# Where one pair's loads stand in the sync engine's queue: an attention and Mish feed-forward kernel in units of three head pairs

## The chip, the cores and the metric

The kernel runs on one core of a Trainium2 chip, and all eight batches are done by that core. The metric is the device time of one execution in microseconds (us), as the median of several runs.

A core has a matrix engine (PE in the profile; PEld is its weight load), a vector engine (DVE), a scalar engine (ACT), a general one (POOL) and a sync engine (SP) that here does nothing but issue DMAs. Each engine works through its own queue in order, and the engines wait for each other through semaphores. All loads of q, k and v, all transposes that are done by DMA and nearly all stores are issued by SP, one behind the other.

## The reference

The kernel computes attention with one extra unit in the denominator of the softmax, and feeds its output, regrouped to one row per token, to a two-layer network with the Mish activation. In and out are float32; B, H, S, D are 8, 12, 448, 64, d_model is 768 and d_ff is 2048.

```
scale = 1.0 / np.sqrt(q.shape[-1])
scores = scale * np.matmul(q, k.transpose(0, 1, 3, 2))
m = np.max(scores, axis=-1, keepdims=True)
e = np.exp(scores - m)
attn = e / (np.sum(e, axis=-1, keepdims=True) + np.exp(-m) + 1e-09)
attn_out = np.matmul(attn, v)

x = attn_out.transpose(0, 2, 1, 3).reshape(B * S, H * D)
h = x @ w_in
g = h * np.tanh(np.log1p(np.exp(h)))      # h itself for the softplus where h > 20
out = g @ w_out
```

## The kernel before, in words

**Pairs and units.** Two heads are a pair; a batch has six pairs, and there are 48. Three pairs are a unit (`UNIT_PAIRS`), two units a batch, so there are 16 units with attention work, u = 0 to 15. The first six pairs (u = 0 and 1) go one by one. The loop `for u in range(UNITS_PER_B, ...)` (line 726) then works on several stages at once: in the pass of unit u it does the scores and exponentials of unit u, the product with v for the pairs of unit u - 1, the first feed-forward product with Mish for part of an earlier batch (`mm1_mish`, L442 and L481), and pieces of the second feed-forward product (`mm2_group`, L548), which fill PE wherever the attention steps wait. In the text a unit is called by its u; the fifth unit is u = 4.

**A pair's way.** `load_pair` (line 149) issues three loads on SP, q, k and v of the pair, 224 KB each (L158), into buffers of which there are four of each kind. `cast_pair` (line 190) casts them to bfloat16 on POOL: q (L201 or L203), k (L207) and v (L188). q and k are then transposed, by PE (`transpose_pair`, L224), or, for the first pair of each unit from pair 21 on and for pair 46, by a DMA on SP (`turn_by_dma`, L237, here called the turn; `TURN_BY_DMA` lists these pairs). The scores (L304, L307, L312) are reduced to maxima by DVE (L335), and ACT takes the exponentials e and their sums (L347). When all e of a unit are there, `normalise` (line 369) divides by the denominator, on DVE (L386), for the third pair of a unit on POOL (L384). It then issues the transpose of that pair's e on SP (L390), so that e can be multiplied by v (`av_pair`, L423).

**A unit's two parts.** The first part is the scores and exponentials. From u = 6 on (`JOINED_FROM`) its order is written out by hand in `JOINED` (line 630): "s" is a score product, "m" the maxima, "e" the exponentials, "fill" a piece of the second feed-forward product, "copy" and "store" its results, "av" and "avc" the product with v of unit u - 1 and its copy, and "cast", "turn" and "load" the steps named above, for the pairs of the next units. The three "av" stand near the end of the order, the one with the third pair (`("av", 2)`) last; score products and exponentials follow behind it. For u = 4 and 5 the orders `GROUPED_LATE_AV` and `LOAD_AT` play that part. The second part is the loop `for f in range(FF_U)` (line 857), eight first feed-forward products with Mish. Between them stand the three normalisations and e transposes of unit u: the first at f = 0, the second at f = 3, the third at f = 4. In the same loop, at f = 1, 3 and 5, PE transposes q and k of those pairs of the next unit that aren't turned by DMA.

**The order on SP in one unit before the change.** For u from 7 on it is: the turn of the next unit's first pair (`("turn", 0)`); the loads of two pairs (`("load", 0)`, p0 + 4, and `("load", 1)`, p0 + 5, where p0 is the unit's first pair); the stores; the loads of one more pair (`("load", 2)`, p0 + 6, the first pair of the unit after the next); and then the three e transposes. `cast_pair` for p0 + 6 stands at the opening of the next unit (`("cast", 0)`). In u = 6 the loads are one pair behind (`lead`), and the pair that closes the row is loaded behind the turn at the end of the order (line 778). In u = 5 the three pairs are loaded at n = 0, 3 and 6 of the first part (line 807).

Of the kernel before, what the change touches and what calls it, by code (L numbers as in the profile page):

```python
# [15 lines left out]
UNIT_PAIRS = 3  # L16
# [3 lines left out]
def kernel(  # L20
# [97 lines left out]
    JOINED_FROM = 2 * UNITS_PER_B + 2  # L118
# [30 lines left out]
    def load_pair(p, which="qkv"):  # L149
        if p >= N_PAIRS:  # L150
            return
        b, h0 = p // HP, (p % HP) * 2
        tiles = loaded.setdefault(p, [])
        for nm, src in (("q", q), ("k", k), ("v", v)):
            if nm not in which:
                continue
            t = ld_pool.tile([SP_, 2, NT * D], FP32, tag=f"{nm}_f", name=f"{nm}_f")
            nc.sync.dma_start(  # L158
                out=t, in_=src[b, h0 : h0 + 2].rearrange("h (p t) d -> p h (t d)", t=NT)
            )  # L160
            tiles.append(t)
# [28 lines left out]
    def cast_pair(p, with_v=True):  # L190
        if p >= N_PAIRS:
            return
        q_f, k_f = loaded[p][:2]
        q_bf, k_bf = (qk_bf[:, p % N_CAST, i] for i in range(2))
        v_bf = bf_pool.tile([SP_, 2, NT * D], BF16, tag="v_bf", name="v_bf")
        by_t = "p h (t d) -> p t h d"
        cast_q, cast_k = nc.gpsimd.tensor_copy, nc.gpsimd.tensor_copy
        if p == 0:
            cast_q, cast_k = nc.vector.tensor_copy, nc.scalar.copy
        if p not in SCALED_IN_CAST:  # L200
            cast_q(out=q_bf, in_=q_f.rearrange(by_t, t=NT))  # L201
        else:
            nc.gpsimd.tensor_scalar(  # L203
                out=q_bf, in0=q_f.rearrange(by_t, t=NT),
                scalar1=SCALE, scalar2=1.0, op0=ALU.mult, op1=ALU.mult,
            )
        cast_k(out=k_bf, in_=k_f.rearrange(by_t, t=NT))  # L207
        casted[p] = (q_bf, k_bf, v_bf)
        if with_v:
            cast_v(p)  # L210
# [32 lines left out]
    def rest_of(p):  # L243
        qT, q_rest = qkT[p][0], q_rests[p % UNIT_PAIRS]
        nc.gpsimd.tensor_copy(out=q_rest[0:64, 0, :], in_=qT[0:64, 384:S])
        nc.gpsimd.tensor_copy(out=q_rest[64:128, 1, :], in_=qT[64:128, 0:64])
# [324 lines left out]
    first_mm2 = 2 * UNITS_PER_B  # L571
# [5 lines left out]
    for g in range(B // 2):  # L577
# [50 lines left out]
        [],  # L628
    )
    JOINED = (  # L630
        ("mA", 1), ("cast", 0), ("fill", 2), ("mA", 0), ("fill", 1), ("mB", 0), ("fill", 1),
        ("eA", 1), ("mB", 1), ("fill", 2), ("eA", 0), ("mB", 2), ("fill", 1), ("eB", 1),
        ("mA", 2), ("fill", 2), ("eB", 0), ("fill", 1), ("copy", 0), ("fill", 3), ("eB", 2),
        ("fill", 3), ("s", 3), ("turn", 0), ("load", 0), ("eA", 2), ("fill", 1), ("m", 3),
        ("s", 5), ("s", 4), ("s", 6), ("mA", 5), ("e", 3), ("fill", 1), ("mA", 6), ("fill", 1),
        ("eA", 5), ("load", 1), ("fill", 1), ("mB", 5), ("fill", 1), ("eA", 6), ("fill", 1),
        ("mB", 4), ("s", 7), ("fill", 2), ("m", 7), ("eB", 4), ("fill", 1), ("mA", 4),
# [18 lines left out]
    BY_POOL = 3  # L656
    LEAD = UNIT_PAIRS + 1
    LOAD_AT = (0, 3, 6)
    TURN_AFTER = (8, 11)
    LAST_AV_AT = 9  # L660
    HEAD = HP
# [64 lines left out]
    for u in range(UNITS_PER_B, N_UNITS + 2 * UNITS_PER_B):  # L726
# [16 lines left out]
        for what, arg in JOINED if joined else ():  # L743
            at, idx = p0 + arg, p0 * STEPS + arg
            heads = {"A": (0,), "B": (1,)}.get(what[-1], (0, 1))
            if what == "s":
                held[arg] = score_products(idx)
            elif what[0] == "m":
                score_maxima(*held[arg], heads)
            elif what[0] == "e":  # L750
                exps(idx, heads)
            elif what == "fill":
                for _ in range(arg):
                    filler.popleft()[0]()
            elif what == "store":
                while to_store:
                    store_rows(*to_store.pop(0))
            elif what == "copy":
                for evac in copies[arg]:
                    evac()  # L760
            elif what == "av":
                held["av", arg] = av_pair(at - UNIT_PAIRS, bank=joined_banks[AV_BANK[arg]])
            elif what == "avc":
                held["av", arg]()
            elif what == "cast":
                if u > JOINED_FROM:
                    cast_pair(nxt)
            elif what == "load":
                lead = LEAD - 1 if u == JOINED_FROM else LEAD
                load_pair(at + lead)  # L770
                if arg:
                    cast_pair(at + lead - 1)
            elif u > JOINED_FROM:
                if nxt + arg in TURN_BY_DMA:
                    turn_by_dma(nxt + arg)
            elif arg:
                turn_by_dma(nxt)
                load_pair(nxt + UNIT_PAIRS)
        if joined:
            expm_of(nxt - 1)  # L780

        for n in () if joined else range(steps):
            pi, s = divmod(n, STEPS)
            p, idx = p0 + pi, p0 * STEPS + n
            late_tp = u == UNITS_PER_B and n == STEPS
            if late_tp:
                transpose_pair(p0 + 2)
            exps(idx)
            if grouped:
                order = GROUPED_LATE_AV if u in LATE_AV else GROUPED  # L790
                flush_late()
                for what, arg in order[n]:
                    if what == "fill":
                        for _ in range(min(arg, len(filler))):
                            fn, w = filler.popleft()
                            fn()
                            done += w
                    elif what in ("av0", "av1"):
                        late.append(av_pair(p0 - UNIT_PAIRS + arg, bank=sc_banks[int(what[2])][0]))
                    else:  # L800
                        flush_late()
                        for i in arg:
                            scores(p0 * STEPS + i)
                if n in LOAD_AT:
                    at = p0 + LOAD_AT.index(n)
                    if u > first_mm2:
                        load_pair(at + LEAD - 1)
                        if n:
                            cast_pair(at + LEAD - 2)
                    elif n < LOAD_AT[-1]:  # L810
                        load_pair(at + LEAD)
                        cast_pair(at + LEAD - 1)
                if u - UNITS_PER_B < len(W_AT):
                    load_w(W_AT[u - UNITS_PER_B].get(n, 0))
                if n in TURN_AFTER and nxt + TURN_AFTER.index(n) in TURN_BY_DMA:
                    turn_by_dma(nxt + TURN_AFTER.index(n))
                continue
            if late_tp:
                evac_qk(p0 + 2, act=True)
            if u == UNITS_PER_B + 1:  # L820
                for i, part in enumerate(TURN_AT[1].get(n, [])):
                    turn_on_pe(*part)
                    if n == 0:
                        mm1_ahead(0, FIRST_AHEAD[i])
            flush_late()
            acc += weight[n]
            want = int(total * acc / sum(weight) + 1e-6)
            while done < want:
                fn, w = filler.popleft()
                fn()  # L830
                done += w
            scores_ahead(end)
            if n in LOAD_AT:
                load_pair(p0 + LOAD_AT.index(n) + LEAD)
                cast_pair(p0 + LOAD_AT.index(n) + LEAD - 1)
            if u - UNITS_PER_B < len(AV_AT):
                early = AV_AT[u - UNITS_PER_B]
                if n in early:
                    late.append(av_pair(early[n], act=early[n] in AV_BY_ACT))
                if u == UNITS_PER_B:  # L840
                    for part in TURN_AT[0].get(n, []):
                        turn_on_pe(*part, act=part in TURN_BY_ACT)
            elif u == N_UNITS and n == LAST_AV_AT:
                for i in range(UNIT_PAIRS):
                    late.append(av_pair(p0 - UNIT_PAIRS + i, bank=sc_banks[i][0]))
            if u - UNITS_PER_B < len(W_AT):
                load_w(W_AT[u - UNITS_PER_B].get(n, 0))
# [9 lines left out]
        for f in range(FF_U):  # L857
# [38 lines left out]
            if f == 3:  # L896
                normalise(todo[1], dma=todo[1] not in BY_PE)
                for p in TURN_BY_DMA:
                    if p // UNIT_PAIRS == u + 1:
                        rest_of(p)  # L900
            if f == 4:
                normalise(todo[2], dma=todo[2] not in BY_PE, on_pool=u + 1 < N_UNITS)
        if attn and u + 1 < N_UNITS:
# [38 lines left out]
```

## Time and profile before

| | |
|---|---|
| median of 3 runs | 459.84 us |
| lowest, highest | 458.76, 463.82 us |
| the profiled execution, its own time | 463.51 us |
| its span, first to last instruction | 461.7 us |
| busy: PE, DVE, ACT, POOL | 430.9, 341.3, 342.0, 185.4 us |
| DMA queue q1 (SP and ACT issue to it) | 85.76 MB, 86.8% of 16 engines' span |
| e transposes by DMA (L390) | 43, median 6.5 us from issue to landing |
| loads of q, k, v (L158) | 48 of each, median 5.1, 5.4 and 5.6 us from issue to landing |

A row of the timeline gives the start in us from the beginning of the span, the duration, the engine, the line of the kernel, the operation, what it writes from what, and how many of one kind were merged; idle time of the engine ahead of it stands in brackets with what ended it. "SPq" is SP's queue; the duration of its rows is the time that the issue holds the queue, not the transfer, which is told by the time to landing. The table of waits gives the time in total, how often, and the longest.

### The profile page before, as it was taken

The page shows a single profiled execution, that of the slowest core. Times are in us where ns is not written, and L with a number is a line of the kernel's source. Part 1 is how long each engine was busy: PE and PEld are TensorE (multiplying, and loading weights), DVE is VectorE, ACT ScalarE, POOL GpSimd, SP SyncE. Part 2 cuts the span into 40 slices and gives each one's busy share as a digit, 9 for nine tenths or more (in the row PEclk, how much of TensorE's full clock was granted, in tenths as well). Part 3 has the DMA queues.
Part 4 walks back from the last instruction along what each step waited for, and adds up shares of the span by engine and source line. Part 5 has one row for each costly group of instructions (what it writes and reads, how often), then busy time and mean ns, then how long its engine had stood idle before and what let it go on. Part 6 is the DMA issues. An engine that isn't in the chain of part 4 may idle for free.

```text
span 461.7 us, 8725 instructions
## 1 busy us (share of the span) xinstructions
PE 430.9 (93%) x2968; PEld 237.4 (51%) x2968; DVE 341.3 (74%) x756; ACT 342.0 (74%) x908; POOL 185.4 (40%) x352
## 2 busy tenths in 40 slices
PE   4587899799999999999999899999999999989996
PEld 2243545454544555555545455565555555555565
DVE  4899777989796888878878888888888888321021
ACT  4998887989696989888878688897978888211300
POOL 3666738462607245453618062535435340000000
PEclk9998589999999999999999999999999999999999
DMA  8999999998999999899999999999999996950213
GB/s 217 219 195 224 256 173 236 200 197 201 203 230 250 222 242 213 258 199 258 220 217 261 198 239 197 277 209 261 230 262 203 233 173 138 177 132 0 70 36 102
DMA packets 211660, 92.65 MB, mean 201 GB/s; under 512 B 168352, under 2 KB 208160, under 8 KB 211616
## 3 DMA queue, kind: packets, MB, share of 16 engines
q1 hardware_dynamic: 204032, 85.76, 86.8%
q0 software_dynamic: 7488, 6.29, 9.4%
q8 instruction: 23, 0.38, 0.3%
q14 instruction: 21, 0.17, 0.1%
q10 hardware_dynamic: 96, 0.05, 0.0%
HBM read 45.61 MB, written 11.01 MB: 123 GB/s over the span
## 4 chain that ended last, share of the span: by engine, by line
PE 69%; DMA 11%; ACT 6%; DVE 6%; issue 2%; SPq 2%; POOL 2%; POOLq 0%; ACTq 0%
PE mo L548 23%; PE mo L442 17%; PE b L442 10%; PE b L304 5%; DMA eT<-en 5%; ACT en L347 5%; DVE negm L335 4%; PE b L548 4%; PE mo L423 3%; DMA k_f<-in_k_dram 3%; DMA v_f<-in_v_dram 2%; PE b L224 2%; PE b L423 2%; SPq L390 1%; DMA q_f<-in_q_dram 1%
## 5 line engine op out<-in xcount | busy, mean ns | idle before, releaser
L347 ACT ACTIVATE en<-b,negm 128x448 bf16<-128x448 f32 x216 | 134.2, 642 | 24.1 <-DVE negm L335 24.1
L335 DVE TENSOR_REDUCE negm<-b 128x1 f32<-128x448 f32 x216 | 121.1, 614 | 15.7 <-PE b L307 15.7
L548 PEld LDWEIGHTS <-gT 128*128 128x128 bf16 x896 | 82.2, 98 | 50.2 <-issue 9.1
L548 PE MATMUL mo<-w_out_sb,gT 128*128 128x384 bf16 (+3 forms) x736 | 107.2, 298 | 0.6 <-ACT gT L481 0.6
L442 PEld LDWEIGHTS <-w_in_sb 128*128 128x128 bf16 x768 | 72.2, 98 | 66.6 <-issue 5.6
L442 PE MATMUL mo<-xT,w_in_sb 128*128 128x448 bf16 x480 | 100.9, 353 | 0.7 <-DVE xT L432 0.3
L384 POOL TENSOR_SCALAR en<-en,rden 128x448 bf16<-128x448 bf16 x109 | 67.5, 640 | 30.3 <-DVE rden L378 23.0
L481 ACT ACTIVATE gT<-mo 128x448 bf16<-128x448 f32 x73 | 40.3, 551 | 52.8 <-PE mo L442 52.6
L386 DVE TENSOR_SCALAR en<-en,rden 128x448 bf16<-128x448 bf16 x227 | 71.7, 385 | 0.7
L442 PE MATMUL b<-xT,w_in_sb 128*128 128x448 bf16 x282 | 58.8, 353 | 0.1
L524 DVE COPY o_sb<-mo 128x384 f32<-128x384 f32 (+3 forms) x54 | 25.8, 492 | 41.6 <-PE mo L548 39.9
L201 POOL CAST qk_bf<-q_f 112x512 bf16<-112x512 f32 x29 | 18.2, 628 | 95.0 <-DMA q_f<-in_q_dram 94.7
L347 ACT ACTIVATE en<-sc,negm 128x448 bf16<-128x448 f32 x84 | 52.6, 644 | 3.9 <-DVE negm L335 2.6
L335 DVE TENSOR_REDUCE negm<-sc 128x2 f32<-128x896 f32 (+1 forms) x48 | 45.4, 968 | 7.0 <-PE sc L307 3.7
L347 ACT ACTIVATION_READ_ACCUMULATOR en<-b,negm 128x1 f32 x216 | 46.2, 214 | 0.0
L188 POOL CAST v_bf<-v_f 112x512 bf16<-112x512 f32 x48 | 30.2, 630 | 17.6 <-DMA v_f<-in_v_dram 15.0
L423 PEld LDWEIGHTS <-v_bf 112*64 112x64 bf16 x384 | 20.8, 112 | 24.0 <-issue 14.4
L207 POOL CAST qk_bf<-k_f 112x512 bf16<-112x512 f32 x47 | 29.1, 620 | 4.9 <-DMA k_f<-in_k_dram 4.0
L423 PE MATMUL mo<-eT,v_bf 112*64 112x448 bf16 x232 | 28.0, 373 | 3.3 <-DMA eT<-en 2.8
L224 PEld LDWEIGHTS <-qk_bf 112*128 112x128 bf16 x304 | 20.2, 106 | 18.3 <-DVE qk_bf L201 4.4
L307 PE MATMUL b<-qk_all 64*128 64x448 bf16 x108 | 29.3, 354 | 0.3 <-ACT en L347 0.3
L304 PE MATMUL b<-qk_all 64*128 64x448 bf16 x108 | 29.3, 354 | 0.0
(71 smaller groups left out, 515.8 us busy)
## 6 DMA issues: line engine op xcount, KB each, us to landing
q_f<-in_q_dram SPq DMA_DIRECT2D x48, 224.0 KB, 5.1
k_f<-in_k_dram SPq DMA_DIRECT2D x48, 224.0 KB, 5.4
v_f<-in_v_dram SPq DMA_DIRECT2D x48, 224.0 KB, 5.6
w_in_sb<-in_moe_w_in_dram POOLq DMA_DIRECT2D x12, 256.0 KB, 5.9
w_out_sb<-in_moe_w_out_dram POOLq DMA_DIRECT2D x8, 384.0 KB, 7.3
out_dram<-o_sb SPq DMA_DIRECT2D x7, 336.0 KB, 5.9
out_dram<-o_sb SPq DMA_DIRECT2D x8, 288.0 KB, 4.9
out_dram<-o_sb SPq DMA_DIRECT2D x8, 240.0 KB, 5.5
```

The source lines that it names most:

```text
L188: nc.gpsimd.tensor_copy(out=casted[p][2], in_=loaded.pop(p)[2])
L224: nc.tensor.transpose(by_s[s][:, t * SP_ : (t + 1) * SP_], src[:, t].rearrange("p h d -> p (h d)"), ident[:SP_, :SP_],)
L304: nc.tensor.matmul(sc[0][:, 0:S], lhsT=qT[0:64, qa : qa + 128], rhs=kA, start=True, stop=True)
L307: nc.tensor.matmul(sc[1][:, 0:S], lhsT=qT[64:128, qb : qb + 128], rhs=kB, start=True, stop=True)
L335: nc.vector.tensor_reduce(out=negm, in_=scored, axis=AX.X, op=ALU.max, negate=True)
L347: nc.scalar.activation(out=st["en"][:, :, c, 0:SP_], in_=sc[bk][:, 0:S].rearrange("q (j c) -> q j c", j=NT), func=AF.Exp, bias=st["negm"][ ...
L384: nc.gpsimd.tensor_scalar(scalar2=1.0, op0=ALU.mult, op1=ALU.mult, **args)
L386: nc.vector.tensor_scalar(scalar2=None, op0=ALU.mult, **args)
L423: nc.tensor.matmul(av[h * 64 : (h + 1) * 64, 0:S], lhsT=v_bf[:, h, j * D : (j + 1) * D], rhs=e_h, start=(j == 0), stop=(j == NT - 1),)
L442: nc.tensor.matmul(h_ps[:, 0:S], lhsT=w_in_sb[:, dm, ff * 128 : (ff + 1) * 128], rhs=xT[b][:, dm, :], start=(dm == 0), stop=(dm == DM_T - 1),)
L481: nc.scalar.activation(out=gT[b][:, ff, :], in_=h_ps[:, 0:S], func=AF.Mish)
L548: nc.tensor.matmul(st["o"][:, st["at"] : st["at"] + nq * NQ], lhsT=src[:, ff, c0 : c0 + 128], rhs=w_out_sb[:, ff, q0 * NQ : (q0 + nq) * NQ ...
```

## The change

From u = 4 on, the loads of the pair `nxt + UNIT_PAIRS` (the first pair of the unit after the next, where `nxt` is the first pair of the next unit) are issued at f = 3 of the unit's second part, behind the second normalisation with its e transpose and ahead of the third. They are taken away where they stood: at n = 0 in u = 5, at `("load", 0)` and at the end of the order in u = 6, and at `("load", 2)`, behind the stores, from u = 7 on. Ten pairs (18, 21, ..., 45) are concerned. The casts of `("load", 2)` stay. The cast of the next unit's first pair moves within the written order from its opening to just ahead of the turn that needs it.

```
-        ("mA", 1), ("cast", 0), ("fill", 2), ("mA", 0), ("fill", 1), ("mB", 0), ("fill", 1),
+        ("mA", 1), ("fill", 2), ("mA", 0), ("fill", 1), ("mB", 0), ("fill", 1),
...
-        ("fill", 3), ("s", 3), ("turn", 0), ("load", 0), ("eA", 2), ("fill", 1), ("m", 3),
+        ("fill", 3), ("s", 3), ("cast", 0), ("turn", 0), ("load", 0), ("eA", 2), ("fill", 1), ("m", 3),
...
+    LOAD_BETWEEN_FROM = first_mm2
...
                 lead = LEAD - 1 if u == JOINED_FROM else LEAD
-                load_pair(at + lead)
+                if arg < 2 and u > JOINED_FROM or arg and u == JOINED_FROM:
+                    load_pair(at + lead)
                 if arg:
                     cast_pair(at + lead - 1)
...
             elif arg:
                 turn_by_dma(nxt)
-                load_pair(nxt + UNIT_PAIRS)
...
                     if u > first_mm2:
-                        load_pair(at + LEAD - 1)
                         if n:
+                            load_pair(at + LEAD - 1)
                             cast_pair(at + LEAD - 2)
...
                 for p in TURN_BY_DMA:
                     if p // UNIT_PAIRS == u + 1:
                         rest_of(p)
+                if u >= LOAD_BETWEEN_FROM:
+                    load_pair(nxt + UNIT_PAIRS)
```

More of the change, by code (lines that the diff above doesn't have):

```diff
@@ L630 @@
     JOINED = (
-        ("mA", 1), ("cast", 0), ("fill", 2), ("mA", 0), ("fill", 1), ("mB", 0), ("fill", 1),
+        ("mA", 1), ("fill", 2), ("mA", 0), ("fill", 1), ("mB", 0), ("fill", 1),
         ("eA", 1), ("mB", 1), ("fill", 2), ("eA", 0), ("mB", 2), ("fill", 1), ("eB", 1),
         ("mA", 2), ("fill", 2), ("eB", 0), ("fill", 1), ("copy", 0), ("fill", 3), ("eB", 2),
-        ("fill", 3), ("s", 3), ("turn", 0), ("load", 0), ("eA", 2), ("fill", 1), ("m", 3),
+        ("fill", 3), ("s", 3), ("cast", 0), ("turn", 0), ("load", 0), ("eA", 2), ("fill", 1), ("m", 3),
         ("s", 5), ("s", 4), ("s", 6), ("mA", 5), ("e", 3), ("fill", 1), ("mA", 6), ("fill", 1),
@@ L658 @@
     LOAD_AT = (0, 3, 6)
+    LOAD_BETWEEN_FROM = first_mm2
     TURN_AFTER = (8, 11)
@@ L769 @@
                 lead = LEAD - 1 if u == JOINED_FROM else LEAD
-                load_pair(at + lead)
+                if arg < 2 and u > JOINED_FROM or arg and u == JOINED_FROM:
+                    load_pair(at + lead)
                 if arg:
@@ L777 @@
                 turn_by_dma(nxt)
-                load_pair(nxt + UNIT_PAIRS)
         if joined:
@@ L806 @@
                     if u > first_mm2:
-                        load_pair(at + LEAD - 1)
                         if n:
+                            load_pair(at + LEAD - 1)
                             cast_pair(at + LEAD - 2)
@@ L900 @@
                         rest_of(p)
+                if u >= LOAD_BETWEEN_FROM:
+                    load_pair(nxt + UNIT_PAIRS)
             if f == 4:
```

## The prediction

> **What bounds the kernel now.** I began with the page, where TensorE is the busiest engine, and then cut the middle of the span into units by the chain that ended last (each unit's run of 32 L548 matmuls marks one) and asked for the busy time of each such stretch.
>
> ```profile
> PE 430.9 (93%) x2968; PEld 237.4 (51%) x2968; DVE 341.3 (74%) x756; ACT 342.0 (74%) x908; POOL 185.4 (40%) x352
> ```
>
> ```profile
> 174.09:198.48 24.39, 24.39 (x174) 13.53 (x175) 20.45 (x48) 20.92 (x57) 11.77 (x24) 1.00 1.01 235
> 198.48:222.88 24.40, 24.40 (x175) 13.62 (x175) 21.49 (x49) 20.93 (x57) 10.33 (x21) 1.00 1.13 231
> 222.88:248.53 25.65, 24.77 (x175) 13.63 (x175) 20.91 (x48) 21.05 (x57) 12.03 (x25) 1.00 1.02 229
> 248.53:274.57 26.04, 24.59 (x174) 13.61 (x175) 21.23 (x49) 20.95 (x57) 10.74 (x22) 1.00 1.07 225
> 274.57:298.97 24.40, 24.40 (x175) 13.54 (x175) 21.15 (x48) 20.93 (x57) 11.18 (x23) 1.00 1.08 231
> 298.97:323.37 24.40, 24.40 (x174) 13.54 (x175) 20.88 (x49) 20.93 (x57) 11.67 (x23) 1.00 1.07 236
> 323.37:348.51 25.14, 24.59 (x174) 13.61 (x175) 21.07 (x48) 20.95 (x57) 11.08 (x23) 1.00 1.14 245
> 348.51:372.56 24.05, 24.05 (x167) 13.24 (x167) 21.28 (x48) 20.55 (x56) 10.42 (x22) 1.00 1.04 201
> ```
>
> After the stretch and its length come PE, PEld, DVE, ACT and POOL busy, the granted clock and the DMA share. A unit takes 24.40 us with PE busy all the time. Nothing that is done for another engine can shorten that. Three stretches are longer, by 1.25, 1.64 and 0.74 us: 3.6 us is all that these eight units have to give back. The waits of PE say what ends most of it: the third product of the normalised e with v (L423, "av 2") waits for its transposed e.
>
> ```profile
> PE mo L423 <- DMA eT<-en: 2.8, 3, 1.5
> ```
>
> ```profile
> 236.39 0.95 PE L423 MATMUL mo<-eT,v_bf 112*64 112x448 bf16 x8 [0.82 <-DMA eT<-en]
> ```
>
> So the question is when the third e transpose of a unit lands. All e transposes, loads, stores and the q/k turn go through SP's one queue. Here it is for unit 7 (u = 7), with the vector engine's end of the first normalise ahead of it:
>
> ```profile
> 191.87 2.59 DVE L386 TENSOR_SCALAR en<-en,rden 128x448 bf16<-128x448 bf16 x7
> ```
>
> ```profile
> 191.68 0.98 SPq L158 DMA_DIRECT2D q_f<-in_q_dram  x1
> 192.71 0.68 SPq L158 DMA_DIRECT2D k_f<-in_k_dram  x1
> 193.43 0.55 SPq L158 DMA_DIRECT2D v_f<-in_v_dram  x1
> ```
>
> ```profile
> 194.52 5.16 SPq L390 DMA_TRANSPOSE eT<-en  x1
> ```
>
> ```profile
> 199.79 4.62 SPq L390 DMA_TRANSPOSE eT<-en  x1
> ```
>
> ```profile
> 204.51 4.68 SPq L390 DMA_TRANSPOSE eT<-en  x1
> 209.30 1.24 SPq L237 DMA_TRANSPOSE qk_all<-qk_bf  x1
> 210.59 0.57 SPq L158 DMA_DIRECT2D q_f<-in_q_dram  x1
> 211.21 0.46 SPq L158 DMA_DIRECT2D k_f<-in_k_dram  x1
> 211.72 0.46 SPq L158 DMA_DIRECT2D v_f<-in_v_dram  x1
> ```
>
> I call the three transposes e0, e1 and e2. e0 starts when the vector engine is done (191.87 + 2.59 = 194.46), not when SP is free (193.98). From there SP is busy issuing without a pause until e2 is out, at 209.19. The time from issue to landing of e2, asked for at 204.51 alone, and the matmuls that use it:
>
> ```profile
> DMA to landing us min/median/max: 6.2/6.2/6.2
> ```
>
> ```profile
> 210.25 1.68 PE L423 MATMUL mo<-eT,v_bf 112*64 112x448 bf16 x16
> ```
>
> e2 lands at 204.51 + 6.2 = 210.7. The row at 210.25 holds two products of eight matmuls, so av 2 starts half way, at 211.1. The slack is 0.4 us. In the unit of 236.39 it is negative already.
>
> **The change part by part.** *The moved loads in units 6 to 13.* The three loads that stood at 191.68 now stand between e1 and e2; eight units do this ahead of an av 2 with so little slack. What is removed, some 2.3 us of SP ahead of e0, is worth little: e0 waited for the vector engine anyway. It is worth something through e0's own issue, which the loads in flight lengthen. Bounds for that: 4.24 us with nothing ahead, in the last unit, and 5.16 as in unit 7.
>
> ```profile
> 392.30 4.24 SPq L390 DMA_TRANSPOSE eT<-en  x1
> ```
>
> I take 4.5 (the stores remain ahead), and 4.3 for e1. With 0.2 of gaps e1's issue is done at 203.5. Then come the three loads, priced by the rows at 210.59: 0.57 + 0.46 + 0.46 and the gaps, 1.6 us. e2 starts at 205.1 instead of 204.5. It lands 6.2 us later if the loads cost it nothing (the row of e2 above), or 8.1 us later as e0 of unit 7 did (asked for at 194.52 alone) with stores and three loads right ahead:
>
> ```profile
> DMA to landing us min/median/max: 8.1/8.1/8.1
> ```
>
> I take 6.8: nearer to the low end, as three loads without stores stand ahead. The landing is then at 211.9 against a due time of 211.1, bounds 211.3 and 213.2. PE waits 0.8 us per unit (0.2 to 2.1), and since scores and exponentials of the next e0 stand behind av 2 on PE, the whole unit slides. The other seven units I take as this one. Eight units: 6.4 us (1.6 to 16.8).
>
> *The waits of before.* All 3.6 us are inside this term's place, so I subtract them. Two of the three waits, however, belong to an e2 that landed late by itself, with only transposes ahead; their times from issue to landing (the e2 issued at 254.8 and that issued at 329.0):
>
> ```profile
> DMA to landing us min/median/max: 7.8/7.8/7.8
> ```
>
> ```profile
> DMA to landing us min/median/max: 7.6/7.6/7.6
> ```
>
> I keep 1.5 us for each of two such landings, since the slack that could hide them is gone: -3.6 + 3.0 = -0.6 (bounds -3.6 and 0).
>
> *The first units.* In u = 4 and 5 av 2 comes far behind its e2, so the extra 1.6 us are hidden there; in u = 5 e2 lands at 152.49 + 6.2 = 158.7 and av 2 starts half way through the second row, at 162.3:
>
> ```profile
> 152.49 4.20 SPq L390 DMA_TRANSPOSE eT<-en  x1
> ```
>
> ```profile
> 161.46 1.68 PE L423 MATMUL mo<-eT,v_bf 112*64 112x448 bf16 x16
> ```
>
>  Pair 18 is loaded sooner, which can remove this wait of the q/k transposes in unit 5:
>
> ```profile
> PE b L224 <- POOL qk_bf L207: 0.5, 2, 0.2
> ```
>
> I book -0.5 (bounds -0.5 and 0).
>
> *The moved cast.* POOL has no other work between its old and its new place in the order, so the move alone costs nothing there. But its load now is issued at 203.5 to 205.1 and not a unit earlier. The turn of unit 8 needs the casts of q and k, and everything behind the turn on SP needs the turn.
>
> ```profile
> L158 SPq DMA_DIRECT2D q_f<-in_q_dram x2: 456/514/571, 210.6 to 212.2; - x2
> ...
> DMA to landing us min/median/max: 3.1/5.2/5.6
> ```
>
> ```profile
> 202.30 0.61 POOL L207 CAST qk_bf<-k_f 112x512 bf16<-112x512 f32 x1
> ```
>
> k, issued at 204.1, lands between 207.2 and 209.7, and its cast ends one or two casts of 0.61 later, 207.8 to 210.9. e2's issue hides it: SP comes to the turn at 205.1 + 4.7 = 209.8. I take 0 (bounds 0 and 1.1 us of SP).
>
> *What is behind e2 on SP.* The turn and two pairs of loads come 209.8 - 209.2 = 0.6 us later. Their last k is cast at 218.39 and used by PE at 219.38:
>
> ```profile
> 218.39 0.63 POOL L207 CAST qk_bf<-k_f 112x512 bf16<-112x512 f32 x1
> ```
>
> ```profile
> 219.38 0.56 PE L224 MATMUL b<-ident,qk_bf 112*128 112x112 bf16 x8
> ```
>
> That leaves 0.36 us, and PE itself arrives 0.8 later, so 0 (bounds 0 and 0.6 per unit). The stores are no longer ahead of a load, which changes nothing on PE.
>
> *The sum:* 6.4 - 0.6 - 0.5 = +5.3 us. Its base is the profiled execution, 463.51 us (span 461.7 and 1.8 around it): 468.8. The median of the three runs shown is 459.84, which is 3.7 lower, about what the waits of this execution come to. On the median the sum gives 465.1; if the median run has no waits to give back it is nearer 459.84 + 6.4 + 3.0 = 469. I take 466, closer to the first.
>
> *A rule beside it.* The loads' 1.6 us of issue is what makes e2 late here. The Trainium skill, page "DMA: Bandwidth & Descriptors", section "Issuing engines are not separate DMA queues", says that the time a sequencer takes to start a DMA is usually small beside the DMA itself. By that the issue term is near 0 and the sum goes to the first rival. The trace agrees only half: 0.5 us of issue against 3.1 to 5.6 us to landing is small, but three of them are more than the slack.
>
> **The rivals.** *The loads are hidden and the waits go (faster).* Place: between e1 and e2. While e2 alone is issued, the DMA engines carry far fewer bytes than when more is in flight:
>
> ```profile
> 203.00:205.00 2.00, 2.00 (x17) 1.10 (x16) 1.83 (x4) 1.78 (x6) 0.47 (x1) 1.00 1.25 275
> 206.00:208.00 2.00, 2.00 (x14) 1.23 (x13) 2.00 (x5) 2.00 (x7) 0.00 (x0) 1.00 1.23 143
> ```
>
> 143 against 275 GB/s leaves room for 0.67 MB of loads (three of 224 KB). It decides if e0 and e1 together take 8.5 us or less and e2 still lands in 6.2: then e2 is there at 194.52 + 8.5 + 0.2 + 1.6 + 6.2 = 211.0, just in time, and the waits of before go: 459.84 - 3.6 - 0.5 = 455.7 at best, 457 with one late landing left. Against it: every one of these values must be at its low end.
>
> *The turn waits for its cast (slower still).* If k lands at 209.7, the turn and six loads wait 1.1 us more on SP, and the q/k transposes of the unit's last pair come 0.5 us after PE's own delay, on top of e2's later landing: with 0.5 to 1 more in each of eight units, 466 + 4 to 8 = 470 to 474. The Trainium skill, the same page, section "Rules for kernel authors", says to issue a DMA early and to wait for it late. By that this rival is the one, as the load now comes later and its cast directly behind it; the trace can't show it before the change, since the load of before had landed long ahead of its cast.
>
> *Nothing changes.* The relief ahead of e0 equals the new issue behind e1. In unit 7 e0 and e1 took 5.16 + 4.62 = 9.78; if they fall to 8.5 and the loads flow at e2's pace, e2 shifts by 0.3 us only, and eight such shifts and the waits of before cancel: 459 to 462. For it speaks that the same bytes pass the same queue.
>
> **How the numbers follow.** Chances: forecast 0.50, loads hidden 0.20, turn waits 0.13, nothing changes 0.17. A measurement of this kernel tells about 1% from no change, that is 4.6 us, 455.2 and 464.4. The forecast's own range, from 0.3 to 1.4 us of wait per unit, is 461 to 471. The overall range goes from 458, which leaves out the better half of the first rival (0.1), to 472, which leaves out the worse half of the second and the upper end of the forecast (0.1). Slower by over 1%: 0.37 of the forecast and all of the second rival, 0.50. Faster by over 1% needs more than all that the waits hold: 0.05. Within 1%: 0.45.
>
> **What would show it.** In the profile of the changed kernel: three L158 issues between the second and third L390 of each unit, 1.6 us together; e0's issue near 4.5; e2 starting about 10.6 us after e0 and landing 6.8 us later; the wait of PE's L423 for eT at 7 to 9 us in about eight places instead of 2.8 in three; units of 25.2 us where 24.40 stood. The forecast is wrong if L423's wait stays under 3 us (then the loads are hidden), or if SP's turn (L237) waits for POOL casts (then the second rival holds). An e2 that starts as early as before shows that the relief ahead of e0 was worth more than I gave it.

## The result, and the profile after

The changed kernel takes 481.27 us (median of 5 runs, 477.96 to 484.79) against 459.84 us before: 1.043 times as long, 95% interval 1.035 to 1.050. The forecast was 466.0 us, between 458 and 472. The direction was right, the size was not.

The profiled execution took 477.96 us, span 476.1. It is the shortest of its five; the profiled execution of before, 463.51, was among the longest of its own. The traces therefore show 14.4 us of the 21 us between the medians; the other 7 us are where these two executions lie among their own kernel's. What the longer executions of the changed kernel do besides was not profiled.

Cut into the same units as in the prediction (length, then PE, PEld, DVE, ACT and POOL busy, the granted clock, the DMA share, and GB/s), the profile of the changed kernel gives:

```profile
172.43:202.90 30.47, 27.21 (x175) 14.29 (x175) 20.77 (x48) 21.24 (x57) 13.48 (x27) 0.89 0.97 208
202.90:227.30 24.40, 24.40 (x176) 13.62 (x175) 20.95 (x49) 20.91 (x57) 9.33 (x19) 1.00 1.03 214
227.30:253.69 26.39, 24.59 (x175) 13.61 (x175) 20.92 (x48) 20.94 (x57) 11.52 (x24) 1.00 1.03 231
253.69:284.43 30.74, 27.60 (x175) 14.40 (x175) 20.66 (x49) 21.27 (x57) 13.04 (x26) 0.89 0.99 196
284.43:308.83 24.40, 24.40 (x174) 13.54 (x175) 20.61 (x48) 20.91 (x57) 9.52 (x20) 1.00 0.96 210
308.83:335.07 26.24, 24.68 (x174) 13.69 (x175) 21.93 (x49) 21.02 (x57) 10.31 (x21) 1.00 1.03 231
335.07:363.22 28.15, 26.28 (x175) 14.02 (x175) 21.13 (x48) 21.15 (x57) 13.59 (x27) 0.94 1.01 219
363.22:387.22 24.00, 24.00 (x166) 13.23 (x167) 21.12 (x48) 20.48 (x56) 8.23 (x17) 1.00 1.11 211
```

The eight units take 214.79 us instead of 198.47. Two things are new. PE idles more, at the place that the prediction named; the waits of PE say so:

```profile
PE mo L423 <- DMA eT<-en: 11.6, 5, 3.3
```

And PE is busy longer in three units, where the granted clock is below 1.00. The longest wait, and the clock around it in short stretches:

```profile
188.38 1.70 PE L423 MATMUL mo<-eT,v_bf 112*64 112x448 bf16 x8 [3.25 <-DMA eT<-en]
```

```profile
186.00:188.00 2.00, 0.00 (x0) 0.00 (x0) 0.40 (x1) 0.00 (x0) 0.00 (x0) 0.78 1.12 86
188.00:193.00 5.00, 4.62 (x17) 1.75 (x17) 2.22 (x4) 1.70 (x5) 1.23 (x2) 0.50 0.97 253
193.00:194.00 1.00, 1.00 (x4) 0.44 (x3) 0.00 (x0) 0.98 (x6) 0.36 (x1) 0.53 1.08 385
194.00:196.00 2.00, 2.00 (x13) 1.00 (x11) 1.92 (x5) 1.99 (x3) 2.00 (x4) 1.00 0.74 288
```

The eight matmuls of av 2 take 1.70 us instead of 0.95, and the clock stays at 0.50 for 6.8 us. SP's queue in unit 7, whose rows of before stand in the prediction:

```profile
197.23 4.22 SPq L390 DMA_TRANSPOSE eT<-en  x1
```

```profile
201.56 4.29 SPq L390 DMA_TRANSPOSE eT<-en  x1
```

```profile
205.90 0.58 SPq L158 DMA_DIRECT2D q_f<-in_q_dram  x1
206.53 0.46 SPq L158 DMA_DIRECT2D k_f<-in_k_dram  x1
207.04 0.73 SPq L158 DMA_DIRECT2D v_f<-in_v_dram  x1
207.87 5.50 SPq L390 DMA_TRANSPOSE eT<-en  x1
213.48 1.23 SPq L237 DMA_TRANSPOSE qk_all<-qk_bf  x1
```

The time from issue to landing of the e2 at 207.87:

```profile
DMA to landing us min/median/max: 7.4/7.4/7.4
```

e0 and e1 are short, as forecast. The three loads hold SP for 2.0 us, and e2 starts 10.6 us after e0. But its issue now takes 5.50 us instead of 4.68, and it lands 7.4 us after its start instead of 6.2: 18.1 us after e0, where 16.2 had been.

**A unit as a loop.** Going from unit to unit there is a closed chain: e0 can go when the first normalisation ends; e2 lands some time later; av 2 waits for it; the last scores stand behind av 2 on PE, their exponentials behind them, and then the next first normalisation. The table takes it from the traces. "Unit" is an eighth of the time from the end of the first normalisation in unit 6 to that in unit 14. "e2 starts" and "e2 lands" are measured from that end too and averaged over units 6 to 13; "issue to landing" is the difference of the two. "Rest" is the unit less the time at which e2 lands. Each row is one profiled execution; names of runs are those of the experiments below.

| kernel | unit | e2 starts | issue to landing | e2 lands | rest |
|---|---|---|---|---|---|
| before | 24.91 | 9.91 | 6.62 | 16.52 | 8.39 |
| changed | 26.88 | 10.82 | 7.67 | 18.49 | 8.40 |
| issue_only | 26.57 | 11.28 | 6.73 | 18.01 | 8.55 |
| ahead_of_second | 26.49 | 11.71 | 6.69 | 18.40 | 8.09 |
| by_pool | 26.41 | 9.16 | 9.09 | 18.25 | 8.17 |
| v_between | 25.89 | 10.26 | 7.14 | 17.40 | 8.48 |
| filled_wait | 27.07 | 10.82 | 7.83 | 18.65 | 8.43 |
| filled_less | 26.94 | 11.05 | 7.57 | 18.62 | 8.32 |
| behind_third | 27.13 | 11.52 | 6.48 | 18.00 | 9.13 |
| scores_first | 25.89 | 11.57 | 7.76 | 19.33 | 6.56 |

In the first eight kernels the rest is 8.1 to 8.6 us, whatever was done to the loads: a unit grows by what e2's landing grows. The changed kernel's e2 lands 1.97 us later, 0.91 from a later start and 1.05 from a slower transfer. Eight units make 15.8 us.

The two traces differ by 1.4 us less than that, since this execution of the changed kernel was 1.5 us ahead of that of before at unit 6. It had been 3.9 us ahead at the first e transpose of unit 4 (112.89 against 116.74), up to which nothing was changed, and lost 2.3 us of it in units 4 and 5. The lead goes with the granted clock early in the span, here in before and then in the changed kernel:

```profile
40.00:62.00 22.00, 18.80 (x125) 10.61 (x126) 17.87 (x31) 17.56 (x51) 17.43 (x28) 0.61 1.18 224
```

```profile
40.00:62.00 22.00, 18.10 (x146) 10.01 (x143) 19.20 (x38) 21.48 (x59) 16.50 (x27) 0.84 1.15 222
```

It stood at 0.50 for 17.1 us there in before and for 6.8 us in the changed kernel. In the fourteen kept traces the first e transpose of unit 3, ahead of which no kernel differs, goes at 89.0 us (3.4 us at 0.50 before it) to 94.6 us (23.9), about 0.3 us later for each microsecond at 0.50. So a spread of 5 to 6 us between executions has nothing to do with the change.

### The profile page after: what moved, and what is told of

Its sections match the earlier page's. It is cut to its first block, busy times and chain, and to the rows that moved or that the text cites. A ratio compares the mean times of both kernels' runs of the same rounds, so it can differ in the third digit from the quotient of the medians.

```text
span 476.1 us, 8726 instructions
## 1 busy us (share of the span) xinstructions
PE 432.4 (91%) x2968; PEld 235.7 (50%) x2968; DVE 340.2 (71%) x756; ACT 342.8 (72%) x908; POOL 185.8 (39%) x352
## 4 chain that ended last, share of the span: by engine, by line
PE 66%; DMA 14%; DVE 7%; ACT 6%; issue 3%; POOL 2%; SPq 1%; POOLq 0%; DVEq 0%
PE mo L548 21%; PE mo L442 17%; PE b L442 11%; DMA eT<-en 11%; ACT en L347 5%; PE b L304 4%; DVE negm L335 4%; PE mo L423 4%; PE b L548 3%; PE b L224 2%; PE b L423 2%; POOL en L384 1%; DMA q_f<-in_q_dram 1%; DVE eT L405 1%; SPq L158 1%
## 5 line engine op out<-in xcount | busy, mean ns | idle before, releaser
L442 PEld LDWEIGHTS <-w_in_sb 128*128 128x128 bf16 x768 | 73.7, 100 | 71.1 <-issue 12.8
L442 PE MATMUL mo<-xT,w_in_sb 128*128 128x448 bf16 x480 | 104.4, 361 | 0.8 <-DVE xT L432 0.3
L386 DVE TENSOR_SCALAR en<-en,rden 128x448 bf16<-128x448 bf16 x227 | 69.5, 375 | 0.7
L442 PE MATMUL b<-xT,w_in_sb 128*128 128x448 bf16 x282 | 61.1, 362 | 0.1
L201 POOL CAST qk_bf<-q_f 112x512 bf16<-112x512 f32 x29 | 18.1, 625 | 79.5 <-DMA q_f<-in_q_dram 79.4
L423 PE MATMUL mo<-eT,v_bf 112*64 112x448 bf16 x232 | 29.0, 379 | 12.2 <-DMA eT<-en 11.6
L203 POOL TENSOR_SCALAR qk_bf<-q_f 112x512 bf16<-112x512 f32 x18 | 11.1, 615 | 57.2 <-DMA q_f<-in_q_dram 57.2
```

Source lines behind the costliest of these rows:

```text
L386: nc.vector.tensor_scalar(scalar2=None, op0=ALU.mult, **args)
L423: nc.tensor.matmul(av[h * 64 : (h + 1) * 64, 0:S], lhsT=v_bf[:, h, j * D : (j + 1) * D], rhs=e_h, start=(j == 0), stop=(j == NT - 1),)
L442: nc.tensor.matmul(h_ps[:, 0:S], lhsT=w_in_sb[:, dm, ff * 128 : (ff + 1) * 128], rhs=xT[b][:, dm, :], start=(dm == 0), stop=(dm == DM_T - 1),)
```

## The experiments

Four theories. Q: e2 is late because the loads' issue stands ahead of it on SP. X: it is late because their bytes travel beside it. C: waits of about 2 us lower the granted clock, and this is a cost of its own. The cast: the turn waits for a cast whose load comes too late (the prediction's second rival). The rows of waits are those of PE from 160 or 165 us, where the pass of unit 6 is under way, to 400 us, the end of the attention work, if not said otherwise; time in total, how often, and the longest.

**issue_only**: the issues without the bytes.

```
+                if JOINED_FROM <= u < N_UNITS - 2:
+                    for t_, src in zip(spare, (q, k, v)):
+                        nc.sync.dma_start(
+                            out=t_, in_=src[0, 0:2, 0:16, :].rearrange("h p d -> p h d")
+                        )
```

> The kernel before, with three small loads (8 KB each, into tiles that nothing reads) issued on SP between the second and third e transpose of units 6 to 13; the real loads stay where they were. So the issues are added without the bytes. Theory Q (queue: the third e transpose, e2, is late because 1.5 us of issue stand ahead of it on SP): e2 starts 10.8 to 11.3 us after e0 and lands 6.2 to 6.6 us after its start, PE waits for it 0.8 to 1.3 us in most of the eight units, 466 to 471 us. Theory X (transfer: e2 is late because the loads' bytes are in flight beside it): e2 is issued later but its landing is covered, 460 to 462 us. By either no wait reaches 1.9 us and the granted clock stays at 1.00.

Measured: 471.7 us, 1.026 (1.019 to 1.033). SP in unit 7:

```profile
201.04 4.21 SPq L393 DMA_TRANSPOSE eT<-en  x1
205.30 0.58 SPq L906 DMA_DIRECT2D spare<-in_q_dram  x1
205.93 0.41 SPq L906 DMA_DIRECT2D spare<-in_k_dram  x1
206.39 0.42 SPq L906 DMA_DIRECT2D spare<-in_v_dram  x1
206.92 4.74 SPq L393 DMA_TRANSPOSE eT<-en  x1
```

```profile
PE mo L426 <- DMA eT<-en: 10.3, 5, 3.2
```

Some 1.6 us of issue, with 24 KB behind it, cost about 11 us over the kernel. Q holds, just above the range it expected (471); X alone is out. That no wait would reach 1.9 us was wrong: they reached 3.2 us, and the clock fell.

**ahead_of_second**: the loads between e0 and e1.

```
+                if u >= LOAD_BETWEEN_FROM:
+                    load_pair(nxt + UNIT_PAIRS)
                 normalise(todo[1], dma=todo[1] not in BY_PE)
...
-                if u >= LOAD_BETWEEN_FROM:
-                    load_pair(nxt + UNIT_PAIRS)
```

> The changed kernel with the moved loads one place earlier on SP, between the first and the second e transpose. The issue ahead of e2 is the same, but the bytes now meet e1, whose product with v comes later. Q: e2 starts 10.5 us after e0 and lands 6.2 to 6.6 us after its start, so at 16.7 to 17.1 instead of the 17.3 to 19.5 of the changed kernel; PE waits 0.5 to 0.9 us per unit, no wait near 2 us, 464 to 469 us. X with engines that are full from e0 to e2: e2 lands at 18 to 18.5 as before the move, 476 to 482 us.

Measured: 478.3 us, 1.040 (1.033 to 1.048). In the table e2 itself is back at 6.69 us from issue to landing, as Q says, but it starts at 11.71: the bytes now make e1's issue longer. In unit 7 e1 and e2 together hold SP for

```profile
202.04 10.01 SPq L390 DMA_TRANSPOSE eT<-en  x2
```

instead of 8.6 without loads in flight (201.56 to 205.85 and 4.3 more). Over the eight units e1's issue takes 5.21 us on average instead of 4.28 in the changed kernel. So X holds in the range that it gave for full engines (a landing at 18 to 18.5 us, 476 to 482 us): a transpose issued right behind 0.67 MB of loads takes about a microsecond longer to issue, and the unit pays this whether it is e1 or e2.

**by_pool**: the bytes without the issue.

```
+                if u >= LOAD_BETWEEN_FROM:
+                    load_pair(nxt + UNIT_PAIRS, queue=nc.gpsimd)
```

(at f = 4 behind the third normalisation, instead of the lines at f = 3)

> The changed kernel with the moved loads issued by POOL, right behind its part of the third normalisation, and not by SP. SP issues the three e transposes without a pause; the bytes still pass while e1 and e2 do. Q: e2 starts 8.7 to 9.2 us after e0, lands at 15.3 to 16.3, PE hardly waits, 456 to 461 us. X: e2 starts as early but takes 7.3 to 8 us to land, so 16.3 to 17; 460 to 467 us, and no wait over 1.5 us.

Measured: 473.9 us, 1.027 (1.021 to 1.033). POOL and SP in unit 7, the time to landing of the e2 issued at 205.34, and the waits:

```profile
202.89 0.71 POOL L158 DMA_DIRECT2D q_f<-in_q_dram  x1
203.59 0.67 POOL L158 DMA_DIRECT2D k_f<-in_k_dram  x1
204.26 0.66 POOL L158 DMA_DIRECT2D v_f<-in_v_dram  x1
```

```profile
205.34 7.10 SPq L390 DMA_TRANSPOSE eT<-en  x1
```

```profile
DMA to landing us min/median/max: 9.2/9.2/9.2
```

```profile
PE mo L423 <- DMA eT<-en: 10.7, 8, 2.0
```

e2 starts earlier than in any other row of the table, 9.16 us, and lands hardly earlier for it (18.25 against 18.49). The loads alone, from POOL's queue, cost about 13 us. Q alone is out too, and X was underestimated: 9.1 us to land where 7.3 to 8 were expected. This isn't a clean price of the bytes: from POOL the loads themselves land later (7.1 to 7.3 us in unit 7, against 3.6 to 5.1 from SP in the changed kernel), and e2 lands later than behind the same loads on SP (9.09 against 7.67). How much is the bytes' and how much POOL's way of issuing them was not separated.

**v_between**: a third of the dose from unit 7 on.

```
+                elif u > JOINED_FROM:
+                    load_pair(at + lead, "qk")
...
-                    load_pair(nxt + UNIT_PAIRS)
+                    load_pair(nxt + UNIT_PAIRS, "v" if u > JOINED_FROM else "qkv")
```

> The changed kernel, but from unit 7 on only the load of v stands between the second and third e transpose; q and k of that pair go back to their old place behind the stores. Units 4 to 6 stay as changed. Q and X alike expect a third of the lateness: e2 starts 9.7 to 10.2 us after e0 and lands at 16.3 to 17, waits of 0 to 0.7 us from unit 7 on, one wait of about 3 us behind unit 6. Theory C (a wait of about 2 us or more makes the granted clock fall to 0.5 for 3.4 or 6.8 us, which costs half of that): one fall, behind unit 6, and none later. 466 to 471 us; without the fall 463 to 467.

Measured: 468.6 us, 1.018 (1.011 to 1.024). One wait of 3.7 us behind unit 6, one fall of the clock, waits of 0.3 to 1.4 later:

```profile
PE mo L423 <- DMA eT<-en: 7.5, 6, 3.7
```

e2's landing moves with the dose. In units 7 to 13, on average, it is 16.69 us with nothing between (before), 17.02 with one load, 18.34 with three (the changed kernel); the 17.40 of the table includes unit 6 with its three loads.

**filled_wait** and **filled_less**: spare matmuls ahead of av 2, eight and four, so that PE isn't idle while it waits. Their result is overwritten by av 2.

```
             elif what == "av":
+                if arg == 2 and u > JOINED_FROM:
+                    for _ in range(8):
+                        nc.tensor.matmul(
+                            joined_banks[AV_BANK[2]][:, 0:S], lhsT=ident,
+                            rhs=w_in_sb[:, 0, 0:S], start=True, stop=True,
+                        )
```

> The changed kernel with eight spare matmuls (128x448, 0.19 us each, their result overwritten) on PE right ahead of av 2 in each unit from 7 on. They run while PE would wait for e2, so they cost nothing where the wait is 1.5 us or more, and they keep PE busy. Theory C (waits of about 2 us make the granted clock fall to 0.5 for 3.4 or 6.8 us): the falls are gone, PE's busy time per unit apart from the spare matmuls is 24.4 again, every unit pays only e2's lateness of some 2 us, 473 to 478 us, and the runs lie closer together than the 478 to 485 of the changed kernel. Without C: the spare work is hidden or adds up to 0.5 us per unit, 480 to 486 us.

> As filled_wait, with four spare matmuls (0.75 us) instead of eight ahead of av 2, so that they fit under nearly every wait for e2 and no longer delay av 2 themselves. Loop theory: no fall of the granted clock, or fewer, and no gain, since a slower PE only hides the next wait: 478 to 485 us like the changed kernel. Theory C, if the eight matmuls hid a gain of it by their own cost: 472 to 477 us.

Measured: 484.35 us, 1.051 (1.045 to 1.057), and 482.93 us, 1.046 (1.043 to 1.050). Units 6 to 13 in one stretch, of the changed kernel first, then with eight and with four spare matmuls:

```profile
168.85:383.93 215.08, 203.46 (x1383) 110.51 (x1381) 168.03 (x381) 168.24 (x449) 89.78 (x176) 0.96 1.01 215
```

```profile
171.47:388.05 216.58, 209.67 (x1445) 114.28 (x1443) 169.70 (x381) 167.73 (x449) 90.73 (x178) 1.00 1.00 214
```

```profile
165.81:381.30 215.49, 204.32 (x1421) 111.58 (x1420) 170.69 (x381) 168.10 (x450) 90.30 (x177) 1.00 1.01 215
```

The falls of the clock in these units are gone with either, so the idle time brings them about, as C says. But nothing is gained. That the spare matmuls delay av 2 by as much as they save is no way out: in filled_less PE still waits for e2 in all eight units,

```profile
PE mo L423 <- DMA eT<-en: 10.7, 8, 1.8
```

and a unit takes 26.94 us against 26.88. A slower PE reaches the next av 2 later, when that unit's e2 has landed: behind 30.47 us comes a unit of 24.40. The loop sets the pace, and the slow clock only takes up time that would have been waited. C as a cost of its own falls, as far as one trace of each kernel shows; of the other executions only the mean clock of the whole span is known (0.972 to 0.993 for filled_less), and it includes the early stretch.

**behind_third**: the loads behind e2, ahead of the turn.

```
-                if u >= LOAD_BETWEEN_FROM:
-                    load_pair(nxt + UNIT_PAIRS)
             if f == 4:
                 normalise(todo[2], dma=todo[2] not in BY_PE, on_pool=u + 1 < N_UNITS)
+                if u >= LOAD_BETWEEN_FROM:
+                    load_pair(nxt + UNIT_PAIRS)
```

> The changed kernel with the moved loads one place later on SP, behind the third e transpose and ahead of the turn. Theories Q and X: neither issue nor bytes stand ahead of e2 now; e2 starts 8.6 to 9.2 us after e0, lands at 15 to 16, and av 2 doesn't wait. The rival of the late cast, which the changed kernel did not show: the turn now has to wait for k to land and be cast, SP reaches it at 18 to 19 us after e0 instead of 16, the six loads behind it come 2 to 4 us late, and PE waits for casts (L224) instead of e2 by 1 to 3 us per unit: 466 to 482 us. If the cast is no limit either: 458 to 462 us.

Measured: 482.8 us, 1.047 (1.041 to 1.053). No wait for e2 is left on PE. Instead, on SP and on PE:

```profile
SPq L237 <- POOL v_bf L188: 27.8, 7, 4.7
```

```profile
PE b L224 <- POOL qk_bf L201: 12.4, 10, 2.3
```

The rival of the late cast is real and as costly, one place later in the queue. In the changed kernel it isn't there: SP waited for a cast at the turn 1.7 us in all.

**first_units**: the loads moved in units 4 and 5 only.

```
-                if u >= LOAD_BETWEEN_FROM:
+                if LOAD_BETWEEN_FROM <= u < JOINED_FROM:
```

(with the old places restored from unit 6 on)

> The loads are moved in units 4 and 5 only; from unit 6 on they stand where they stood before. It prices the first part of the change by itself. From the two traces units 4 and 5 lost 1.6 us at av 2 and 0.8 us at casts: 461 to 465 us. If the first units are free, as the prediction had it, 458 to 461.

Measured: 461.74 us, 1.001 (0.998 to 1.005). The first units are free; the 2.3 us that the changed kernel's trace lost in units 4 and 5 aren't in these medians. The moved cast stands in this kernel in every unit from 6 on, so it is free by itself too.

**scores_first**: the changed kernel with the last scores taken out from behind av 2.

```
-        ("av", 2), ("avc", 0), ("mB", 8), ("s", 9), ("mB", 9), ("avc", 2), ("eB", 9), ("mA", 9),
+        ("s", 9), ("av", 2), ("avc", 0), ("mB", 8), ("mB", 9), ("eB", 9), ("mA", 9), ("avc", 2),
```

> The changed kernel with the order of the unit's end altered: score product 9 goes ahead of av 2 on PE, and the copy of av 2 goes behind the maximum of 9 on DVE. e2's lateness after e0 is left as it is (18 to 18.5 us). If PE's in-order wait at av 2 is what makes the whole unit slide, because the last scores, their exponentials and so the next e0 stand behind it, then the next e0 no longer slides with it, the lateness is paid once and not in every unit, the waits at av 2 shrink to under 1 us and the clock stays up: 462 to 470 us. If e2's lateness costs PE the same wherever the scores stand: 477 to 484 us.

Measured: 473.5 us, 1.027 (1.021 to 1.033), 7.8 us less than the changed kernel although e2 lands later still after e0 (19.33). The rest falls from 8.40 to 6.56: this is the loop shortened at its other end, and it supports that PE's order behind av 2 makes the unit slide. The gain was smaller than expected (462 to 470 us), since e2 lands 0.84 us later and gives half of it back; and the waits at av 2 didn't shrink to under 1 us, they are 7.5 us in five, the longest 2.0.

**before with scores_first**, **loads_ahead_of_stores** (on before, the pair's loads ahead of the stores) and **both**: three attempts at a kernel faster than before.

```
-("copy", 2), ("store", 0), ("load", 2)
+("copy", 2), ("load", 2), ("store", 0)
```

> The kernel before with the unit's end reordered as in the run scores_first: score product 9 ahead of av 2 on PE, the copy of av 2 behind the maximum of 9 on DVE; all loads where they stood before. Loop theory (a unit lasts as long as e0 to the landing of e2 and on through av 2 and the last scores to the next e0, whenever that is longer than PE's own 24.4 us): before pays this in three or four units, 3.6 us in the profiled execution; taken out of the loop they shrink, 457 to 461 us against 459 to 462. If the later copy of av 2 is waited for by the next feed-forward product, each unit loses up to 0.6 us: 462 to 466.

> The kernel before with the pair's three loads one place earlier in the first part of the unit: ahead of the stores instead of behind them, still ahead of e0. The opposite direction of the change. Loop theory: nothing is added between e0 and e2, so it can't be slower than before by more than the spread; the unit whose e0 was late because SP stood at these loads (by 1.6 us in the profile of before) gets better: 457 to 461 us. If the stores, now next to e0, lengthen its issue as the loads did: the same time as before, 459 to 462.

> Both edits of the two runs above on the kernel before. If each gives what the loop theory says and they don't overlap: 455 to 460 us; if both take the same waits, as the better of the two.

Measured: 463.0, 462.5 and 463.0 us against 461.3 for before, measured beside them: 1.0046 (1.0008 to 1.0084), 1.0038 (1.0003 to 1.0072), 1.0045 (1.0013 to 1.0077). None helps, and none comes to the 461 us or less that the loop let one hope for. Before is left with 0.5 us per unit over PE's 24.40, so there was little to win; why even that didn't come was not found out. No version beat it.

## Why the prediction went wrong, point by point

**Right.** The place (av 2 waiting for e2), the direction, the worth of the relief ahead of e0 (e0 and e1 took 4.22 + 4.29 us in unit 7 against 4.5 + 4.3), e2's start in unit 7 (10.64 us after e0, forecast 10.6), the hidden cast (SP waited for casts at the turn 1.7 us in all), the free first units, and that the whole unit slides with av 2.

**The step that failed: the term of the moved loads.** Its mechanism was right and its size was not: 0.8 us per unit, 6.4 in the sum, where 1.97 and 15.8 were measured. The 0.8 was a start 0.6 us later, a transfer 0.6 us slower, less 0.4 of slack. On the mean of the eight units it is 0.91, 1.05 and nothing, so the three parts failed by 0.3, 0.45 and 0.4 us.

**Wrong: e2's issue to landing.** The prediction took 6.8 us, "nearer to the low end, as three loads without stores stand ahead". It was 7.67 on average and 7.4 in unit 7, where the row of e0 in unit 7 of before, 8.1 us, had shown what loads in flight do. The stores were no reason to go lower: in the changed kernel three loads without stores were enough to hold up a transpose by a microsecond, and so they were ahead of e1 in ahead_of_second.

**Wrong: unit 7 for all.** In unit 7 e2 had 0.4 us of slack. On the mean of the eight units of before e2 landed at 16.52 and the unit was 24.91, 0.5 us over 24.40. In filled_less, where PE waits for e2 in every unit and the clock doesn't fall, the rest has no slack in it, and it is 8.32; before's 8.39 is hardly more. So there was no slack on the mean, and every microsecond of lateness counted in full.

**Wrong: the waits of before as a credit.** The -0.6 was in the same place; in the loop they are part of the 24.91. And of the 3.6 us only 2.8 were waits of av 2.

**Not shown: the step from 468.8 to 466.** The prediction put the 3.7 us between the profiled execution and the median down to its waits. The traces show another reason for executions to differ that is as large, the clock early in the span.

**Missing: the granted clock.** Its falls were not foreseen. By filled_wait and filled_less they cost nothing more in these units.

**The rivals.** "Hidden" is out: the room of 143 against 275 GB/s did not let the loads pass for nothing: with them in flight e2's issue takes longer (4.68 to 5.50 us in unit 7). What holds it up inside the transfer was not measured. "Nothing changes" is out. The late cast did not happen here and does in behind_third. The Trainium skill, page "DMA: Bandwidth & Descriptors", section "Issuing engines are not separate DMA queues", calls the issue time usually small beside the DMA itself. That holds for each load here (0.5 to 0.7 us of issue in unit 7 against 3.6 to 5.1 to landing), but it was no measure of the cost: issue_only shows three such issues costing about 11 us over the kernel.

**Open.** In the traces the loop gives 15.8 us; the medians differ by 21. And the two costs do not add: the issues alone came to 10.7 us, the loads from POOL to 12.9, both to 20 or 21, and per unit in the traces to 1.66, 1.50 and 1.97 us. Part of this is the relief ahead of e0, which issue_only doesn't have (e2 starts at 11.28 there, 10.82 in the changed kernel), and part may be that by_pool overstates the bytes; the rest was not separated.

## What to carry to other kernels

Before a transfer is put between others in a queue, look for the chain that leads from the queue's first item round to itself in the next round, and add up its length; if it is as long as the round, each microsecond put in it is paid every round, whatever the busiest engine. Loads put ahead of a DMA transpose cost twice here, by their issue and by lengthening the transpose, and moving them to POOL's queue saved the first and not the second. One unit's slack is not the slack: take the mean over all of them, and the worst.

## What the runs showed of the hardware that was not expected

**How a wait lies decides whether the clock falls.** In the changed kernel it fell after three of five waits, those of 3.25, 3.14 and 1.87 us, and not after those of 1.80 and 1.56; it stayed at 0.50 for 6.8, 6.8 and 3.4 us. The length of the wait alone doesn't decide: in ahead_of_second the clock stayed at 1.00 after one of 2.69 us. Between 100 and 430 us the falls of every trace begin on a grid with a step of 3.41 us. Counted by steps of that grid, over the fourteen traces, a fall followed on each of the thirteen steps in which PE was idle for 1.87 us or more, and on none with 1.79 or less. The step with 1.87 in the changed kernel, the one with 1.79 in filled_less, and the two that share the wait of 2.69 in ahead_of_second (step less PE busy is the idle time):

```profile
347.55:350.96 3.41, 1.54 (x15) 0.62 (x11) 1.45 (x4) 0.60 (x2) 0.00 (x0) 1.00 1.02 221
```

```profile
289.57:292.98 3.41, 1.62 (x14) 0.77 (x12) 1.24 (x3) 0.39 (x2) 0.00 (x0) 1.00 1.02 191
```

```profile
262.76:266.18 3.42, 2.11 (x20) 0.97 (x21) 3.31 (x6) 2.06 (x8) 0.00 (x0) 1.00 1.43 192
266.18:269.59 3.41, 2.03 (x15) 1.00 (x15) 0.72 (x2) 0.06 (x1) 0.00 (x0) 1.00 0.80 219
```

The Trainium skill, page "TensorE: Matmul & The Clock Gate", Part 1, gives an idle window of about 3.4 us for such a fall; here 1.87 us of idle time inside 3.41 us were enough.

**A fetch of instructions may make a transpose late.** The prediction met two e2 in before that landed 1.4 to 1.6 us late "by themselves". The DMA queues in the time of the one issued at 254.79 show a packet that those of the e2 at 230.12 don't have, on the queue of kind "instruction" (packets, MB, share of 16 engines):

```profile
q1 hardware_dynamic: 5447, 1.38, 116.6%
q8 instruction: 1, 0.02, 0.8%
```

It is a packet of 16 KB, and it came 5.8 us after the issue, near the end of the transfer; the one of the e2 at 329.0 came after 5.3 us. Of the six late e2 of this kind in before, the changed kernel and issue_only (units 6, 9 and 12), all had such a packet 5.3 to 6.4 us after their issue; e2 with a packet in the first 2.2 us, or none, landed 1.0 to 1.9 us sooner. It isn't always so: in behind_third (unit 9) and filled_less (unit 14) an e2 with such a packet after 5.5 and 5.6 us landed in 6.1 and 6.2. That the packet delays the transfer is inferred from its time; no run took it away.
